# The end of attention's first batch in a fused attention and mixture-of-experts kernel: last steps packed closer, token weights moved behind them, a third output tile begun early

## The chip, the cores and the metric

The kernel runs on one core of a Trainium2 chip. A core has a matrix engine (TensorE, PE in the rows; PEld are its weight loads), three elementwise engines (VectorE, DVE; ScalarE, ACT; GpSimd, POOL) and a queue that issues transfers (SyncE, SP). Each works through its own list in order and waits on semaphores for the others. The metric is the device time of one execution in microseconds (us), the median of several runs.

## The reference

Attention over 2 batches of 8 heads, 576 positions, head size 64: heads 0 to 3 see the last 32 positions ("local"), heads 4 to 7 every 32nd ("strided"). Its output, as a matrix of 1152 tokens by 512, goes through four experts and a gated layer:

```python
attn_out = _attn_ref(**attn_kwargs)                 # softmax(q k^T / 8, masked) v
x = attn_out.transpose(0, 2, 1, 3).reshape(B * S, H * D)
p = domain_probs / (domain_probs.sum(-1, keepdims=True) + 1e-09)
for e in range(E):
    out += p[:, e:e+1] * (np.maximum(x @ w1[e], 0.0) @ w2[e])
gate = 1 / (1 + np.exp(-(out @ w_gate)))
return (gate * (out @ w_val) @ w_out)
```

All is float32. The kernel keeps a float32 value as two parts that TensorE takes, a high and a low one, and makes a product of three matmuls: high by high, low by high, high by low.

## The kernel before

**Attention in groups.** `attention` makes 16 groups of one batch, half a head each (kind `s` strided or `l` local, `c` the pair of heads, `half`, `hh` the head in the pair). A group goes through scores and mask on TensorE (tile `sps`), a row maximum on VectorE (`nm`), the exponentials on ScalarE (`P`, with the row sums in `sm`), the norm (two short VectorE operations on `sm`, a `TENSOR_SCALAR` and a `RECIPROCAL`, and a multiplication of `P` on GpSimd), a transposition on TensorE (`tps`) with a copy to `PT` on VectorE, and the product with the values on TensorE (`o`), for two groups at a time. The split takes `o` apart into the high part `xh` (a `CAST`) and the low part `xl` (a subtraction) of x, separately for each tile of 384 tokens. The software pipeline is by steps: group n starts at step n, `STAGES` (L46) says how many steps later each stage comes, and `attention` emits what falls into a step, stage by stage. The order of the stages in a step is that of `STAGES`, values first. `DRAIN` (L51) is the number of empty steps between the two batches.

**Buffers.** `o` has a PSUM bank of its own, one; only the last local `o` of each batch (half 1, c 1) is taken from the pool `gp`. That pool has four banks (`PSUM_BUFS`, L33), which also hold `tps`, `qkps` (transposed q and k), `warm`, `pps` and the output tiles `gps`.

**Split and weights.** From step `WEIGHTS_FROM` (L50) to `FIRST_GROUPS` both halves of a split are on VectorE; in other steps ScalarE copies `o` to `of` first and GpSimd makes the low part. From that step the weights of the first layer are prepared as well, one `early_step` or two behind each group: ScalarE casts 512 columns (`wh`), GpSimd subtracts (`wl`).

**The seam.** After the first 21 steps the units begin: `early_up` of the first tile of tokens makes four output tiles (fb 0 to 3) of 12 matmuls, over four blocks of x (kk); blocks 2 and 3 are strided heads, 0 and 1 local ones. `head_start` makes the six matmuls of blocks 2 and 3 in advance, at steps 17 and 18 (`HEAD_START`), for two of the four tiles. `keep_warm` puts matmuls on zeros into TensorE's list (`EMPTY`: how many in which step). `token_weights` and `spread_token_weights` normalise the token weights `ptok`, transpose them (`pps`), store them to DRAM (`pd`) and load them spread over the partitions (`p00`, first used by `early_down`). In the units, attention's second batch goes on between the matmuls: every product of three counts 0.36 of a step (`ATT_RATE`), so the places are fixed by the program's text, not by time.

Of the kernel before, what the change touches and what calls it, by code (L numbers as in the profile page):

```python
# [9 lines left out]
F32 = mybir.dt.float32  # L10
# [7 lines left out]
ALU = mybir.AluOpType  # L18
# [14 lines left out]
PSUM_BUFS = 4  # L33
PB_BUFS = 5
WARM = 11
EMPTY = {0: 2, 1: 4, 2: 2, 3: 2, 4: 2, **{i: 2 for i in range(5, 16, 2)}, 16: 1, 19: 1, 20: 1}
T_BUFS = 4
STEP_US = dict(early_up=0.53, early_down=0.53, expert_up=0.49, expert_down=0.49, gated_up=0.25, gated_down=0.65)
MARGIN = 5.5
# [5 lines left out]

STAGES = (("values", 5), ("transpose", 3), ("scores", 0), ("exp", 0), ("norm", 1), ("split", 5))  # L46
QUAD = 4
FIRST_GROUPS = 21
PT_BUFS = 5
WEIGHTS_FROM = 12  # L50
DRAIN = 5  # L51
HEAD_START = (17, 18)
ATT_RATE = 0.36


# [51 lines left out]
def attn_moe_glu_kernel(ctx, tc, q, k, v, dp, w1, w2, wg, wv, wo, out):  # L107
    nc = tc.nc
    ledger = Ledger()
    dve, act, pool_ = (Reckoned(e_, name, ledger) for e_, name in ((nc.vector, "V"), (nc.scalar, "A"), (nc.gpsimd, "G")))  # L110
    B, H, S, D = q.shape
# [8 lines left out]
    NU = S // 8  # L120
# [42 lines left out]
    def load_strided_v(b, c):  # L163
        h0 = 4 + 2 * c
        t = atp.tile([NU, 2, 8 * D], F32, tag="vs", name="vs", bufs=2)
        nc.sync.dma_start(t, v[b, h0:h0 + 2].rearrange("h (u r) d -> u h (r d)", r=8))
        qkv["vs", b, c] = t
# [38 lines left out]
    for e in range(EARLY // 2, E):  # L206
        for w_, name in ((w1, "w1"), (w2, "w2")):
            parts = []
# [11 lines left out]
    at = prep_order.index(item_of["wo", 0])  # L220
# [69 lines left out]
    def token_weights():  # L290
        dve.tensor_reduce(psums, ptok, AX.X, ALU.add)
        dve.tensor_scalar(psums, psums, 1e-9, None, ALU.add)
        dve.reciprocal(psums, psums)
        dve.tensor_tensor(ptok, ptok, psums.unsqueeze(2).to_broadcast([128, NTB, E]), ALU.mult)

    def spread_token_weights():
        ps = gp.tile([128, 512], F32, tag="g", name="pps")
        nc.tensor.transpose(ps[:NTB * E, :128], ptok.rearrange("p t e -> p (t e)"), ident)
        t = atp.tile([128, 288], F32, tag="PT", name="ptokT", bufs=PT_BUFS)
        ptokT = t[:NTB * E, :128]  # L300
        dve.tensor_copy(ptokT, ps[:NTB * E, :128])
        nc.sync.dma_start(pd, ptokT)
        load_p(0, 0, p00)
# [3 lines left out]
    def load_p(e, T, t):  # L307

        m = TC // 128
        src = pd.rearrange("(t e) p -> e t p", e=E)[e, m * T:m * T + m, :]  # L310
        nc.sync.dma_start(t, bass.AP(src.tensor, src.offset, [[0, 128], [E * 128, m], [1, 128]]))
        pb[e, T] = t.rearrange("p a b -> p (a b)")


    xh, xl = {}, {}
# [5 lines left out]
    def x_parts(b, lo, hi):  # L321

        done = lo
        while done < hi:
            T, o = divmod(b * S + done, TC)
            n = min(hi - done, TC - o)
            yield T, o, done, n
            done += n
# [336 lines left out]
    pt_tiles, of_tiles, soft = {}, {}, {}  # L665

    def qk_strided(b, c, hhs):

        for hh in hhs:
            for nm, dst in (("qs", QT), ("ks", KT)):  # L670
                src, t = qkv[nm, b, c], atp.tile([128, 4, NU], F32, tag=nm + "T", name=nm + "T", bufs=3)
                dst["s", b, c, hh] = t
                ps = gp.tile([128, 512], F32, tag="g", name="qkps")
                pv_ = ps[:, :4 * NU].rearrange("p (a b) -> p a b", b=NU)
                for rp in range(4):
                    nc.tensor.transpose(  # L676
                        pv_[:, rp, :], src[:, hh, rp * 128:(rp + 1) * 128], ident[:NU, :NU]
                    )
                if nm == "qs":
                    act.activation(t, pv_, AF.Copy, scale=SCALE)  # L680
                else:
                    dve.tensor_copy(t, pv_)
        if hhs[-1] == 0:
            return
        if (b, c) == (0, 1):
            alloc_x(NT - 1)
        if (b, c) == (1, 1):
            acc["x2"] = accp.tile([128, KC, NTOK], F32, tag="acc", name="x2acc")
# [73 lines left out]
    def group_values(g):  # L762
# [10 lines left out]
        for j in range(m):  # L773
            for x in range(2):
# [7 lines left out]
                )  # L782
        if at_step[0] in range(WEIGHTS_FROM, FIRST_GROUPS):
            of_tiles[g] = o, o
# [2 lines left out]
        act.copy(of, o[:, :288])  # L787
        of_tiles[g] = o, of

    def group_split(g):  # L790

        kind, b, c, half, hh = g
        if hh == 0:
            return
        o, of = of_tiles.pop(g)
        low = dve if of is o else pool_
        if kind == "s":
            kk = 2 + c
            hv, ov = (t[:, :288].rearrange("p (a u) -> p a u", u=NU) for t in (o, of))
            for T, off, s0, n in x_parts(b, 0, S):  # L800
                u0, u1 = s0 // 8, (s0 + n) // 8
                sel = lambda t: t[T][:, kk, off:off + n].rearrange("p (u a z) -> p z a u", a=4, z=2)[:, half]
                dve.tensor_copy(sel(xh), hv[:, :, u0:u1])
                low.tensor_tensor(sel(xl), ov[:, :, u0:u1], sel(xh).bitcast(F32), ALU.subtract)
        else:
            for T, off, s0, n in x_parts(b, 288 * half, 288 * half + 288):
                p0 = s0 - 288 * half
                dh, dl = xh[T][:, c, off:off + n], xl[T][:, c, off:off + n]
                dve.tensor_copy(dh, o[:, p0:p0 + n])
                low.tensor_tensor(dl, of[:, p0:p0 + n], dh.bitcast(F32), ALU.subtract)  # L810

    at_step = [0]

    def attention():

        gs = []
        for b in range(B):
            gs += [("s", b, c, half, hh) for c in range(2) for hh in range(2) for half in range(2)]
            gs += [("l", b, c, half, hh) for half in range(2) for hh in range(2) for c in range(2)]
        n = len(gs)  # L820
        stage = dict(values=group_values, transpose=group_transpose, scores=pair_scores,
                     exp=group_exp, norm=group_norm, split=group_split)

        def later(x):
            return int(x % QUAD == QUAD - 1 and (x + 1) % (n // B) != 0)

        step_of = [x + DRAIN * (x // (n // B)) for x in range(n)]
        at_stage = {}
        for name, behind in STAGES:
            for x in range(n):  # L830
                if name in ("values", "split"):
                    if x % QUAD >= 2:
                        at_stage[name, step_of[x] + behind + later(x)] = gs[x]
                elif name == "scores":
                    if x % 2 == 0:
                        at_stage[name, step_of[x]] = gs[x:x + 2]
                else:
                    at_stage[name, step_of[x] + behind] = gs[x]
        qk_strided(0, 0, (0,))
        for i in range(step_of[-1] + STAGES[-1][1] + 1):  # L840
            at_step[0] = i
            for name, _ in STAGES:
                if (name, i) in at_stage:
                    stage[name](at_stage[name, i])
            if i == 0:
                qk_strided(0, 0, (1,))
            if i in HEAD_START:
                head_start(HEAD_START.index(i))
            if i in EMPTY:
                keep_warm(EMPTY[i])  # L850
            for b in range(B):
                at = i - step_of[b * n // B]
                if b and at in (-5, -3):
                    qk_strided(b, 0, (int(at == -3),))
                if at in (2, 3):
                    qk_strided(b, 1, (at - 2,))
                if at in (6, 7, 9):
                    qk_local(b, (6, 7, 9).index(at))
            yield i
# [21 lines left out]
    def head_start(fb):  # L881

        head[fb] = g_tile()[:, :TC]
        for _ in split_products(head[fb], early_pairs(0, 0, fb, (2, 3)), last=False):
            pass
# [326 lines left out]
    def early_step(n):  # L1212
        ledger.now = max(ledger.now, ledger.done)
        prep_step(n)
# [28 lines left out]
    with tc.manual_schedule():  # L1243
# [12 lines left out]
        def attend():  # L1256

            i = next(att, None)
            if i == 0:
                load_strided_qk(1, 0)  # L1260
                load_raw_to(2)
            if i == 6:
                load_raw_to(3)
                load_strided_qk(1, 1)
            if i == 9:
                load_strided_v(1, 0)
            if i == 11:
                load_local(1)
            if i == 13:
                load_strided_v(1, 1)  # L1270
            if i == 18:
                token_weights()
            if i == 19:
                spread_token_weights()
            if i == 20:
                load_vl(1)
            return i

        att = attention()
        for i in range(FIRST_GROUPS):  # L1280
            attend()
            for _ in range((i >= WEIGHTS_FROM) + (i > 15)):
                early_step(0)
        n_none, n_step = 0, [0]
        halves = job(x_half())
# [103 lines left out]
```

## Time and profile before

| | us |
|---|---|
| runs | 650.26, 650.40, 650.83 |
| median | 650.40 |
| the profiled execution's own time | 651.06 |
| its span, first to last instruction | 648.9 |
| TensorE busy in it | 638.2 (98%) |

A row of the timeline has the start in us from the span's start, the time, engine, line, operation, output and input tiles, shape and count; in square brackets the idle time just before it and who ended it. The end of a matmul is modelled, and matmuls overlap, so the distance of two starts says more than the time of one. Line L101 is a helper that records every operation of VectorE, ScalarE and GpSimd, so those are told apart by their tiles.

### The profile page before, as it was taken

Reading aid. Unit: us, or ns where it says so; the run is one execution under the profiler, and the core shown is the slowest. Engines: PE = TensorE matmul, PEld = TensorE weight load, DVE = VectorE, ACT = ScalarE, POOL = GpSimd, SP = SyncE. Lnnn points to the kernel's source line nnn. Section 1 sums busy time; section 2 is a strip of 40 time slices with the busy share of each in tenths; the row PEclk is TensorE's granted clock in tenths of the full one; section 3 lists DMA queues with packets and bytes.
Section 4 is the critical chain, followed back from the end, with each engine's and each line's share of the span. In section 5 each row is a group of like instructions: output and inputs, shape, how many; then the busy total and the mean of one; then the engine's idle time right before and its main releaser. Section 6 shows DMA issues by size and latency. Waiting matters only on the chain.

```text
span 648.9 us, 12702 instructions
## 1 busy us (share of the span) xinstructions
PE 638.2 (98%) x4899; PEld 469.3 (72%) x4904; DVE 440.3 (68%) x885; ACT 341.7 (53%) x807; POOL 265.5 (41%) x307
## 2 busy tenths in 40 slices
PE   8889999999999999999999999999999999999998
PEld 5668889999676666666666666666979877987794
DVE  4876586787461886693887788898866659633432
ACT  5747553554854646774645554642565574532230
POOL 3665561000422226361335335440465377453540
PEclk9999999999999999999999999999999999999999
DMA  9965141030421544251664464354113832330002
GB/s 184 243 172 141 35 117 43 1 115 17 142 86 57 158 147 159 81 182 59 183 255 143 163 227 147 98 162 146 35 34 117 286 142 81 107 132 1 33 19 97
DMA packets 48884, 77.00 MB, mean 119 GB/s; under 512 B 19540, under 2 KB 24440, under 8 KB 47672
## 3 DMA queue, kind: packets, MB, share of 16 engines
q1 hardware_dynamic: 48824, 76.20, 37.6%
q8 instruction: 38, 0.62, 0.4%
q14 instruction: 22, 0.18, 0.1%
HBM read 59.66 MB, written 16.53 MB: 117 GB/s over the span
## 4 chain that ended last, share of the span: by engine, by line
PE 94%; DVE 1%; DMA 1%; SPq 1%; ACT 1%; issue 0%; POOL 0%; POOLq 0%; ACTq 0%
PE gps L874 23%; PE gps L876 23%; PE gps L875 23%; PE gps L976 19%; SPq L173 1%; PE sps L730 1%; PE warm L264 1%; PE tps L756 1%; PE o L780 1%; DMA ks<-in_k_dram 1%; ACT P L101 1%; DMA kl<-in_k_dram 1%; PE qkps L698 0%; PE qkps L676 0%; PE sps L717 0%; DVE nm L101 0%
## 5 line engine op out<-in xcount | busy, mean ns | idle before, releaser
L101 POOL TENSOR_TENSOR hl<-t,hh 128x384 f16<-128x384 f32 x72 | 76.5, 1065 | 179.2 <-ACT t L101 175.4
L976 PEld LDWEIGHTS <-w 128*128 128x128 f16 x1512 | 125.0, 98 | 1.8
L976 PE MATMUL gps<-x,w 128*128 128x192 f16 x1512 | 126.2, 246 | 0.0
L874 PE MATMUL gps<-x,w 128*128 128x384 f16 x288 | 93.9, 326 | 0.0
L875 PE MATMUL gps<-x,w 128*128 128x384 f16 x288 | 93.9, 326 | 0.0
L876 PE MATMUL gps<-x,w 128*128 128x384 f16 x288 | 93.9, 326 | 0.0
L874 PE MATMUL gps<-hh,w 128*128 128x384 f16 x288 | 93.9, 326 | 0.0
L875 PE MATMUL gps<-hl,w 128*128 128x384 f16 x288 | 93.9, 326 | 0.0
L876 PE MATMUL gps<-hh,w 128*128 128x384 f16 x288 | 93.9, 326 | 0.0
L874 PEld LDWEIGHTS <-w 128*128 128x128 f16 x576 | 56.4, 98 | 37.3 <-issue 0.2
L876 PEld LDWEIGHTS <-w 128*128 128x128 f16 x576 | 56.4, 98 | 37.2
L875 PEld LDWEIGHTS <-w 128*128 128x128 f16 x576 | 56.4, 98 | 36.4
L101 ACT ACTIVATE hh<-gps 128x384 f16<-128x384 f32 (+1 forms) x96 | 46.8, 487 | 48.8 <-PE gps L876 48.5
L101 POOL TENSOR_TENSOR stage<-magn,stage 128x512 f16<-128x512 f32 x36 | 45.5, 1273 | 45.1 <-ACT magn L101 38.9
L101 ACT ACTIVATE w<-raw,up 128x512 f16<-128x512 f32 x48 | 32.0, 715 | 34.8 <-DVE up L101 34.7
L101 ACT ACTIVATE P<-sps,nm 72x72 f32<-72x72 f32 (+1 forms) x112 | 36.4, 333 | 23.8 <-DVE sm L101 17.0
L101 ACT ACTIVATE bits<-raw 128x512 f32<-128x512 f32 x36 | 24.3, 674 | 38.1 <-DVE magn L101 37.9
L101 DVE SCALAR_TENSOR_TENSOR w<-raw,up,w 128x512 f16<-128x512 f32 x48 | 40.1, 871 | 5.1 <-ACT w L101 4.9
L101 POOL TENSOR_TENSOR sg<-four,sg 128x384 f32<-128x384 f32 x9 | 9.6, 1069 | 80.8 <-DVE four L101 77.9
L874 PE MATMUL gps<-w,hh 128*128 128x512 f16 (+1 forms) x112 | 41.6, 371 | 0.0
L875 PE MATMUL gps<-w,hh 128*128 128x512 f16 (+1 forms) x112 | 41.6, 371 | 0.0
L876 PE MATMUL gps<-w,hl 128*128 128x512 f16 (+1 forms) x112 | 41.6, 371 | 0.0
(145 smaller groups left out, 1281.5 us busy)
## 6 DMA issues: line engine op xcount, KB each, us to landing
raw<-in_moe_w_dram SPq DMA_DIRECT2D x32, 512.0 KB
raw<-in_moe_w_gate_dram SPq DMA_DIRECT2D x12, 512.0 KB
raw<-in_moe_w_val_dram SPq DMA_DIRECT2D x12, 512.0 KB
raw<-in_moe_w_out_dram SPq DMA_DIRECT2D x12, 512.0 KB
wg<-stage SPq DMA_DIRECT2D x21, 256.0 KB
wv<-stage SPq DMA_DIRECT2D x21, 256.0 KB
w<-wg SPq DMA_DIRECT2D x3, 1024.0 KB
wo<-stage SPq DMA_DIRECT2D x12, 256.0 KB
```

The lines of the kernel that those rows point to most:

```text
L101: return f(*a, **k)
L173: nc.sync.dma_start(t[:, :, j, :], src[b, 2 * j:2 * j + 2].rearrange("h s d -> (h s) d").rearrange("(c p) d -> p c d", p=128),)
L264: nc.tensor.matmul(ps, zero.to_broadcast([128, 128]), zero.to_broadcast([128, 512]), start=True, stop=True,)
L730: nc.tensor.matmul(pv_[:, j, :], qs_, ks_, start=False, stop=j == m - 1)
L756: nc.tensor.transpose(pv_[:, j, :], pp[:, j, :], ident[:n, :n])
L780: nc.tensor.matmul(o[x * 64:x * 64 + 64, j * n:(j + 1) * n], lhsT, tts[x][:, j, :], start=True, stop=True)
L874: nc.tensor.matmul(ps, ah, bh, start=first and i == 0, stop=False)
L875: nc.tensor.matmul(ps, ah, bl, start=False, stop=False)
L876: nc.tensor.matmul(ps, al, bh, start=False, stop=last and i == n - 1)
L976: nc.tensor.matmul(o, l_, r_, start=first and x + kk + y == 0, stop=last and x * kk * y == 2, skip_group_check=True)
```

## The change

- The first batch's last groups are packed. The `o` of c 1, half 0 comes one step after that of c 0 (step 16, not 17), the two of half 1 both in step 18 (not 19 and 20), the two last transpositions in steps 16 and 17. `DRAIN` goes from 5 to 3 and `FIRST_GROUPS` from 21 to 19.
- `group_split` takes several groups and goes by tiles of tokens first: the parts of the first 384 tokens of both `o`, then the rest.
- Three tiles are begun in advance, two in step 17 and one in step 18.
- Token weights are made in step 20 and spread in step 21, inside the first unit. The load of the second batch's local values (`vl`) moves from step 20 to 18.
- `WEIGHTS_FROM` goes from 12 to 11, so that the split of step 11 moves wholly to VectorE; weight preparation starts a step earlier and skips step 15: ten steps up to the units, where there were fourteen.
- The warm-up matmuls of steps 19 and 20 go, step 16 has two for one.
- The strided q and k of the second batch are transposed three and one steps ahead of it (five and three before): steps 16 and 18 as before.

```diff
-EMPTY = {0: 2, 1: 4, 2: 2, 3: 2, 4: 2, **{i: 2 for i in range(5, 16, 2)}, 16: 1, 19: 1, 20: 1}
+EMPTY = {0: 2, 1: 4, 2: 2, 3: 2, 4: 2, **{i: 2 for i in range(5, 17, 2)}, 16: 2}
-FIRST_GROUPS = 21
+FIRST_GROUPS = 19
-WEIGHTS_FROM = 12
-DRAIN = 5
-HEAD_START = (17, 18)
+WEIGHTS_FROM = 11
+DRAIN = 3
+HEAD_START = {17: (0, 1), 18: (2,)}
...
+    def group_split(*gs):
...
+        tiles = [of_tiles.pop(g) for g in gs]
+        for T, off, s0, n in parts:
+            for g, (o, of) in zip(gs, tiles):
+                low = dve if of is o else pool_
...
+                dve.tensor_copy(sel(xh), src(o))
+                low.tensor_tensor(sel(xl), src(of), sel(xh).bitcast(F32), ALU.subtract)
...
+        m = n // B
+        for name, x, i in (("values", m - 5, m), ("split", m - 5, m), ("transpose", m - 2, m), ("transpose", m - 1, m + 1),
+                           ("values", m - 2, m + 2), ("values", m - 1, m + 2), ("split", m - 2, m + 2), ("split", m - 1, m + 2)):
+            at_stage = {k_: g for k_, g in at_stage.items() if k_[0] != name or g != gs[x]}
+            moved.append((name, i, gs[x]))
...
-            if i in HEAD_START:
-                head_start(HEAD_START.index(i))
+            for fb in HEAD_START.get(i, ()):
+                head_start(fb)
...
-                if b and at in (-5, -3):
-                    qk_strided(b, 0, (int(at == -3),))
+                if b and at in (-3, -1):
+                    qk_strided(b, 0, (int(at == -1),))
...
+            if i == 20:
+                token_weights()
+            if i == 21:
+                spread_token_weights()
             if i == 18:
-                token_weights()
-            if i == 19:
-                spread_token_weights()
-            if i == 20:
                 load_vl(1)
...
-            for _ in range((i >= WEIGHTS_FROM) + (i > 15)):
+            for _ in range((i >= WEIGHTS_FROM) + (i > 15) - (i == 15)):
                 early_step(0)
```

TensorE's list at steps 15 to 17, before (-) and after (+); `qkps` are the second batch's q and k, and the row ahead of this piece is the `tps` of step 15, ahead of that the `o` of c 0, half 0:

```order
 L264 MATMUL warm<-const-float32-0.0 128x512
-L756 MATMUL tps<-ident,P 128x96 x3
+L780 MATMUL o<-PT,vl 64x96 x6
+L756 MATMUL tps<-ident,P 128x96 x6
+L264 LDWEIGHTS const-float32-0.0
+L264 MATMUL warm<-const-float32-0.0 128x512
 L264 LDWEIGHTS const-float32-0.0
 L264 MATMUL warm<-const-float32-0.0 128x512
 L676 MATMUL qkps<-ident,qs 128x72 x4
 L676 MATMUL qkps<-ident,ks 128x72 x4
-L780 MATMUL o<-PT,vl 64x96 x6
 L756 MATMUL tps<-ident,P 128x96 x3
```

The second `o` now stands ahead of the transposition, the warm-up and the eight `qkps` matmuls that stood between it and the first.

VectorE's list at steps 11 and 12, before:

```order
L101 CAST xh0_171<-o_575 128x4x48
L101 CAST xh1_173<-o_575 128x4x24
L101 COPY PT_619<-tps_615 128x288
L101 TENSOR_REDUCE nm_631<-sps_621 96x3
L101 TENSOR_SCALAR sm_593<-sm_593 96x3
```

and after:

```order
L101 CAST xh0_171<-o_575 128x4x48
L101 TENSOR_TENSOR xl0_172<-o_575,xh0_171 128x4x48
L101 CAST xh1_173<-o_575 128x4x24
L101 TENSOR_TENSOR xl1_174<-o_575,xh1_173 128x4x24
L101 COPY PT_620<-tps_616 128x288
L101 TENSOR_REDUCE nm_632<-sps_622 96x3
L101 TENSOR_SCALAR sm_591<-sm_591 96x3
```

Two subtractions came in ahead of the copy, the maximum and the sums. GpSimd's list over steps 11 to 15, before:

```order
L101 TENSOR_TENSOR xl0_172<-of_584,xh0_171 128x4x48
L101 TENSOR_TENSOR xl1_174<-of_584,xh1_173 128x4x24
L101 TENSOR_TENSOR P_594<-P_594,sm_593 96x384
L101 TENSOR_TENSOR P_633<-P_633,sm_632 96x384
L101 TENSOR_TENSOR wl_642<-raw_230,wh_641 128x512
L101 TENSOR_TENSOR P_661<-P_661,sm_660 96x384
L101 TENSOR_TENSOR P_697<-P_697,sm_696 96x384
L101 TENSOR_TENSOR wl_642<-raw_230,wh_641 128x512
```

and after:

```order
L101 TENSOR_TENSOR P_592<-P_592,sm_591 96x384
L101 TENSOR_TENSOR wl_614<-raw_230,wh_613 128x512
L101 TENSOR_TENSOR P_634<-P_634,sm_633 96x384
L101 TENSOR_TENSOR P_660<-P_660,sm_659 96x384
L101 TENSOR_TENSOR wl_614<-raw_230,wh_613 128x512
L101 TENSOR_TENSOR P_696<-P_696,sm_695 96x384
```

The two subtractions left it, and each `wl` stands one norm earlier.

TensorE's list at the end of the last tile begun in advance, before (the second tile, step 18):

```order
L874 MATMUL gps_794<-xh0_171,wh_641 128x384
L875 MATMUL gps_794<-xl0_172,wh_641 128x384
L876 MATMUL gps_794<-xh0_171,wl_642 128x384
L676 MATMUL qkps_802<-ident_97,qs_226 128x72 x4
L676 MATMUL qkps_809<-ident_97,ks_227 128x72 x4
L780 MATMUL o_824<-PT_717,vl_164 64x96
L780 MATMUL o_824<-PT_775,vl_164 64x96
```

and after (the third tile, step 18; both `o` of half 1 stand ahead of it, `gps_784` is tile 0 going on):

```order
L888 MATMUL gps_822<-xh0_171,wh_613 128x384
L889 MATMUL gps_822<-xl0_172,wh_613 128x384
L890 MATMUL gps_822<-xh0_171,wl_614 128x384
L676 MATMUL qkps_830<-ident_97,qs_226 128x72 x4
L676 MATMUL qkps_837<-ident_97,ks_227 128x72 x4
L888 MATMUL gps_784<-xh0_171,wh_613 128x384
```

The two `qkps` now come when three tiles begun in advance and one `o` hold `gp`'s four banks; before, two tiles held two.

## Rows read from the trace of the kernel before

**Rows 1.** Busy us (instructions) by stretch: PE, PEld, DVE, ACT, POOL; granted clock, DMA, GB/s.
```profile
25.00:70.00 45.00, 39.56 (x402) 32.82 (x404) 32.19 (x94) 27.66 (x124) 27.67 (x32) 1.00 0.62 160
70.00:640.00 570.00, 570.00 (x4227) 417.74 (x4226) 391.03 (x738) 297.20 (x597) 226.89 (x251) 1.00 0.34 112
```
**Rows 2.** TensorE's timeline, 29 to 45 us.
```profile
29.84 0.60 PE L264 MATMUL warm<-const-float32-0.0 128*128 128x512 bf16 x2
31.07 0.47 PE L756 MATMUL tps<-ident,P 96*128 96x96 f32 x3 [0.63 <-POOL P L101]
...
32.89 0.72 PE L780 MATMUL o<-PT,vl 128*64 128x96 f32 x12 [0.20 <-PE sps L730]
...
33.84 0.38 PE L264 MATMUL warm<-const-float32-0.0 128*128 128x512 bf16 x1
34.95 0.47 PE L756 MATMUL tps<-ident,P 96*128 96x96 f32 x3 [0.72 <-POOL P L101]
...
35.72 0.41 PE L676 MATMUL qkps<-ident,ks 72*128 72x72 f32 x4
36.23 0.72 PE L780 MATMUL o<-PT,vl 128*64 128x96 f32 x12
...
38.85 0.47 PE L756 MATMUL tps<-ident,P 96*128 96x96 f32 x3 [0.42 <-POOL P L101]
39.10 0.42 PE L874 MATMUL gps<-xh,wh 128*128 128x384 f32 x1
...
40.24 0.41 PE L676 MATMUL qkps<-ident,qs 72*128 72x72 f32 x4
40.49 0.42 PE L676 MATMUL qkps<-ident,ks 72*128 72x72 f32 x4
...
43.15 0.27 PE L298 MATMUL pps<-ident,ptok 128*36 128x128 f32 x1 [1.26 <-DVE ptok L101]
...
44.36 0.38 PE L264 MATMUL warm<-const-float32-0.0 128*128 128x512 bf16 x1 [0.29 <-DVE ptokT L101]
```
**Rows 3.** VectorE's timeline, 28 to 53 us.
```profile
28.07 0.65 DVE L101 CAST xh<-o 128x192 fp32r<-128x192 f32 x2
28.55 0.44 DVE L101 COPY PT<-tps 128x288 f32<-128x288 f32 x1
...
31.17 0.47 DVE L101 CAST xh<-o 128x192 fp32r<-128x192 f32 x1
...
32.70 0.45 DVE L101 COPY PT<-tps 128x288 f32<-128x288 f32 x1
...
34.97 0.17 DVE L101 TENSOR_SCALAR sm<-sm 96x3 f32<-96x3 f32 x1
...
35.72 0.46 DVE L101 TENSOR_TENSOR xl<-o,xh 128x288 fp32r<-128x288 f32 x1
...
36.52 1.07 DVE L101 TENSOR_SCALAR sm<-sm 96x3 f32<-96x3 f32 x1
...
42.92 0.24 DVE L101 CAST xh<-o 128x96 fp32r<-128x96 f32 x1
...
44.03 0.27 DVE L101 COPY ptokT<-pps 36x128 f32<-36x128 f32 x1
...
52.78 0.56 DVE L101 SCALAR_TENSOR_TENSOR hl<-gps,hh 128x384 fp32r<-128x384 f32 x1 [1.53 <-ACT hh L101]
```
**Rows 4.** GpSimd's timeline, 29 to 38 us.
```profile
29.10 1.08 POOL L101 TENSOR_TENSOR xl<-of,xh 128x192 fp32r<-128x192 f32 x2
30.19 0.82 POOL L101 TENSOR_TENSOR P<-P,sm 96x384 f32<-96x384 f32 x1
...
36.29 1.28 POOL L101 TENSOR_TENSOR wl<-raw,wh 128x512 fp32r<-128x512 f32 x1
```
**Rows 5.** ScalarE's timeline at 40.7 us: the copy of transposed q out of `qkps`.
```profile
40.69 0.41 ACT L101 ACTIVATE qsT<-qkps 128x288 f32<-128x288 f32 x1 [2.94 <-PE qkps L676]
```
**Rows 6.** TensorE's timeline at the start: the first eleven warm-up matmuls.
```profile
0.78 4.81 PE L264 MATMUL warm<-const-float32-0.0 128*128 128x512 bf16 x11 [0.78 <-PEq L1374]
```

More of the change, by code (lines that the diff above doesn't have):

```diff
@@ L788, in group_values @@
         of_tiles[g] = o, of
-    def group_split(g):
-        kind, b, c, half, hh = g
-        if hh == 0:
+    def group_split(*gs):
+        for kind, b, c, half, hh in gs:
+            break
+        else:
             return
-        o, of = of_tiles.pop(g)
-        low = dve if of is o else pool_
         if kind == "s":
[L798 to L804, printed above, removed]
-        else:
[L806 to L810, printed above, removed]
+            parts = x_parts(b, 0, S)
+        else:
+            parts = x_parts(b, 288 * half, 288 * half + 288)
+        tiles = [of_tiles.pop(g) for g in gs]
+        for T, off, s0, n in parts:
+            for g, (o, of) in zip(gs, tiles):
+                low = dve if of is o else pool_
+                if kind == "s":
+                    kk, u0, u1 = 2 + g[2], s0 // 8, (s0 + n) // 8
+                    sel = lambda t: t[T][:, kk, off:off + n].rearrange("p (u a z) -> p z a u", a=4, z=2)[:, half]
+                    src = lambda t: t[:, :288].rearrange("p (a u) -> p a u", u=NU)[:, :, u0:u1]
+                else:
+                    p0 = s0 - 288 * half
+                    sel = lambda t: t[T][:, g[2], off:off + n]
+                    src = lambda t: t[:, p0:p0 + n]
+                dve.tensor_copy(sel(xh), src(o))
+                low.tensor_tensor(sel(xl), src(of), sel(xh).bitcast(F32), ALU.subtract)
     at_step = [0]
@@ L827, in attention @@
         step_of = [x + DRAIN * (x // (n // B)) for x in range(n)]
-        at_stage = {}
+        at_stage, moved = {}, []
         for name, behind in STAGES:
@@ L844, in attention @@
                     stage[name](at_stage[name, i])
+                both = [g for name_, i_, g in moved if (name_, i_) == (name, i)]
+                if name == "split":
+                    group_split(*both)
+                else:
+                    for g in both:
+                        stage[name](g)
             if i == 0:
                 qk_strided(0, 0, (1,))
-            if i in HEAD_START:
-                head_start(HEAD_START.index(i))
+            for fb in HEAD_START.get(i, ()):
+                head_start(fb)
             if i in EMPTY:
```

## The prediction, as put on record

> **What bounds the kernel now.** Read the windows first [rows 1]. From 70 us TensorE is busy 570.00 of 570.00 us at a granted clock of 1.00, so nothing that another engine does there sets the end, and the three products of every value are the same matmuls before and after. What the change can win or lose lies ahead of 70 us: TensorE is busy 39.56 of 45 us between 25 and 70. All of the idle time gone would be 5.4 us, the most that can be won there, and each microsecond added there goes through to the end, since no idle time is left behind it to take it up. The chain of waits that ended last says the same: it is matmuls nearly all the way, so I read TensorE's timeline next [rows 2], and for each idle time in brackets the engine that ended it [rows 3 to 5].
>
> The reader should see three kinds of wait there. The transpositions `tps` at 31.07, 34.95 and 38.85 us wait for GpSimd's norm (0.63, 0.72, 0.42 us). The `o` at 36.23 starts 0.05 us after VectorE's subtraction on the same bank ended (35.72 + 0.46 = 36.18), and 0.26 us later than the matmuls ahead of it would have let it (35.72 + 0.25, the distance of the two `qkps` at 40.24 and 40.49). And `pps` waits 1.26 us for the token weights, the `warm` behind it 0.29 us.
>
> **What the change takes away.** The warm-ups fall from four to three in these steps, and two pairs differ from one by 0.60 - 0.38 = 0.22 us: 0.22. The waits of `pps` and the `warm` behind it leave this place: 1.26 + 0.29. The wait of the `o` in front of its bank (0.26) and those of the two `tps` (0.72 and 0.42) go because the waits below stand ahead of them or in their place. Together 3.17 us.
>
> **What it adds, step by step.**
>
> Step 11. VectorE had two casts ahead of the copy `PT`, 28.55 - 28.07 = 0.48 us; now it has casts and subtractions, which cost 32.70 - 31.17 = 1.53 us one split later [rows 3]. Everything behind them (maximum, sums, norm, transposition) is 1.05 us later. In return GpSimd loses 1.08 us of `xl`, which the norm `P` at 30.19 had waited behind [rows 4]. The relief only helps if `P` is not then waiting for VectorE; its input comes from the list that has just become longer. Between 0 and 1.05; I take 0.7, nearer the price of the four operations.
>
> VectorE behind `wl`. A `TENSOR_SCALAR` on `sm` costs 0.17 us at 34.97 and 1.07 us at 36.52, and the second lies inside GpSimd's `wl` (36.29 to 37.57) and ends with it [rows 3, 4]. The subtraction of 0.46 us at 35.72, out of PSUM, is not stretched. After the change each `wl` stands one norm earlier, right behind the `P` that VectorE's own previous sums released: it runs from about 0.9 to 2.2 us behind those sums (a `P` of 0.82, then 1.28), and the next group's sums (36.52 - 34.97 = 1.55 us apart here) fall into it at steps 13 and 15. Each can lose 0 to 1.1 us; for the pair 0 to 2.2, I take 1.5, since the one case seen lost 0.9. The Trainium skill, page "SBUF — State Buffer", section "Who interferes with whom", says that VectorE and GpSimd share a port pair that one instruction holds to its end, and that `tensor_scalar` can need it, while an operation with one SBUF input outside the two-port modes does not. By that rule both meetings cost in full and the sum would be 0.7 us more; the two rows agree with it.
>
> The second `o`. All local `o` but the last share one bank. The next one waits until VectorE has taken the one before apart. Start of `o` to end of `xl` was 36.18 - 32.89 = 3.29 us [rows 2, 3]. Before, a `tps`, two `warm`, another `tps` and eight `qkps` stood between. Now there is `o` and `tps` (33.84 - 32.89 = 0.95 us) and two warm-ups of 0.22: 1.39 us. The wait is 1.9 us, 1.7 at the least if VectorE comes a little sooner. This is the term I trust most: the bank is one, the place in the list is given.
>
> The transposition of step 17. It needs the norm of a group whose sums come only a step earlier, and VectorE's list is now 1 to 2 us late while TensorE has less to do ahead of it. The nearest rows are waits of 0.42 to 0.72 us with the old distance [rows 2]; a step nearer, the whole chain of sums, reciprocal and `P` (0.17 + 0.17 + 0.82) shows. 0.9 to 1.3, I take 1.1.
>
> Four banks. Three tiles begun in advance and the one `o` of step 18 hold all of `gp`. The first `qkps` behind them waits until VectorE has taken both `o` apart, in eight operations; four cost 44.03 - 42.92 = 1.11 us, so about 2.3 us from the end of the first `o`. TensorE has under it the second `o` and the third tile's six matmuls (40.24 - 39.10 = 1.14 us), so 0.5 to 1.1 us are open. The second `qkps` has again no free bank and waits for ScalarE's copy of the first, 0.41 us [rows 5] and the ways there and back, 0.4 to 0.7. Sum 0.9 to 1.8, I take 1.6.
>
> `pps` in the unit. Moved to the first unit it takes a bank that is released only by a low part `hl`, and `hl` at 52.78 stands behind a wait of 1.53 us for ScalarE [rows 3]. What TensorE loses of that is between 0.3 and 1.5; I take 0.9, the middle, since no row is nearer to either end.
>
> Weights. With ten preparation steps for fourteen, at least two `wl` of 1.28 us go into the first units, where GpSimd also has the norms of the second batch. Hidden if the units' matmuls ahead cover them, else up to half of the pair: 0 to 1.3, I take 0.5. `vl` earlier and the token weights' transfers behind the weight loads on SyncE cost nothing as long as the first use of `p00`, in `early_down`, is later than their landing; the DMA engines' share is 0.62 in this stretch and 0.34 behind it [rows 1], so there is room, and I price it at 0 and leave its failure to the range.
>
> The sum: 0.7 + 1.5 + 1.9 + 1.1 + 1.6 + 0.9 + 0.5 = 8.2 added, 3.17 removed: 5.0 us net. The profiled execution took 651.06 us, 0.66 more than the median of the runs, 650.40. So 656.1 against that execution, and 655.4 on the runs' basis. All low ends give 0 + 0 + 1.7 + 0.9 + 0.9 + 0.3 + 0 = 3.8, net 0.6; all high ends 1.05 + 2.2 + 1.9 + 1.3 + 1.8 + 1.5 + 1.3 = 11.05, net 7.9.
>
> **The rivals.** *Faster.* The second `o` hardly waits. Its bank is free once the cast and the subtraction, twice some 0.46 us, have followed the end of the first `o` (0.72 us after its start): 1.64 us, if VectorE had nothing else to do, against 1.39 us of work ahead, a wait of 0.25. If VectorE's list is ahead by then (GpSimd's relief at step 11 outweighs the four operations, no sums fall into a `wl`), then the other waits stand at their low ends too: 0.25 + 0.5 for the transposition + 0.9 + 0.3 = 1.95, less 3.17, net -1.2: 649.2. It decides at an added sum under 3.17. Against it: VectorE reached that cast at about 35.72 - 0.46 = 35.26, some 1.65 us after the `o` ended (32.89 + 0.72), with a copy and sums ahead of it (34.97), and its list has become longer, not shorter. Chance 0.08.
>
> *No difference.* The change does what it says in the order of the lists, but waits only change places: the 5.4 us of idle time are spread over fewer steps, the sums miss `wl`, the banks come free in time. That is near the low ends, net -1.3 to +1.3: 650.4. The windows speak for it so far as the matmuls are the same; the two structural waits (second `o`, banks) speak against. Chance 0.06.
>
> *Slower still, by the clock.* The granted clock is 1.00 through waits of up to 1.26 us. The first eleven warm-ups, at the start, took 4.81 us, 0.44 each [rows 6], and later 0.22: the level of 1.2 GHz for that of 2.4. A gap of 1.9 us or more, with waits of about 1 us on both sides, has no row here. If the clock falls there, the `o`, `tps`, warm-ups and `qkps` behind it, some 2.2 us, and perhaps the tiles begun in advance take double: 2 to 4 us, I take 3: 658.4. The Trainium skill, page "TensorE: Matmul & The Clock Gate", section "HAM oscillation — how this bites in real kernels", describes such a fall behind idle stretches; the trace of before shows none. Chance 0.10.
>
> **How the numbers follow.** My forecast, net +5.0, has 0.76, so 655.4 us. The range is to hold the time 8 times in 10: from 652.2 (between the sum of low ends, 651.0, and the forecast) to 657.8 (the high ends give 658.3, part of the clock's rival lies within). Left out are the faster and the equal rival (0.14) and the upper half of the clock's. A measurement here can tell about 0.2%, 1.3 us, from no change. Slower by more than that: 0.76 + 0.10 = 0.86; within it 0.06; faster 0.08.
>
> **What would show it.** In the new trace TensorE should be idle nearly 2 us or more ahead of the `o` of step 16, ended by VectorE's `xl`; one or two `TENSOR_SCALAR` on `sm` of about 1 us should lie inside a `wl`; the first `qkps` behind the third tile should wait about 1 us and the second 0.5 us or so; `pps` should wait for `hl`; and from about 75 us TensorE should again be busy throughout. If the `o` of step 16 starts without a wait, the largest term is wrong and with it the sign may be; if the clock shows less than 1.00 behind it, the third rival holds.

## The result, and the profile after

The changed kernel took 660.3 us (659.7 to 661.2 in four executions), before 650.6 in the same comparison: a ratio of 1.0149, interval 1.0131 to 1.0166. It is 9.7 us slower. The direction was forecast, the size was not: 5.0 us were forecast, and the time lies above the range (652.2 to 657.8).

The profiled execution took 660.36 us, with a span of 658.5 against 648.9. Read its windows beside [rows 1]; the columns are the same.

```profile
25.00:70.00 45.00, 35.67 (x318) 29.04 (x317) 27.66 (x81) 21.94 (x96) 20.83 (x23) 0.89 0.60 158
70.00:110.00 40.00, 38.51 (x353) 32.94 (x353) 26.62 (x77) 21.45 (x92) 23.98 (x31) 1.00 0.26 78
110.00:640.00 530.00, 530.00 (x3915) 386.89 (x3915) 365.27 (x676) 280.32 (x531) 206.24 (x221) 1.00 0.35 115
```

Two things are new. TensorE is idle 9.3 us between 25 and 70 us, where it was 5.4, and another 1.5 between 70 and 110. And the granted clock between 25 and 70 us is 0.89, not 1.00. From 110 us on TensorE is busy throughout, so all that is lost lies ahead of that; the forecast had this from about 75 us on, and the wait of 1.39 us at 81.72 lies behind that.

TensorE's timeline of the changed kernel, the rows with a wait of 0.5 us or more and two rows behind the longest; to be read against [rows 2].

```profile
30.31 0.72 PE L780 MATMUL o<-PT,vs 72*64 72x72 f32 x16 [0.86 <-DVE xl L101]
...
35.34 0.72 PE L780 MATMUL o<-PT,vl 128*64 128x96 f32 x12 [1.41 <-issue]
...
39.77 1.23 PE L780 MATMUL o<-PT,vl 128*64 128x96 f32 x12 [2.88 <-DVE xl L101]
40.92 1.22 PE L756 MATMUL tps<-ident,P 96*128 96x96 f32 x6
...
43.97 0.74 PE L756 MATMUL tps<-ident,P 96*128 96x96 f32 x3
...
51.34 0.44 PE L676 MATMUL qkps<-ident,qs 72*128 72x72 f32 x4 [0.81 <-DVE xl L101]
52.28 0.47 PE L676 MATMUL qkps<-ident,ks 72*128 72x72 f32 x4 [0.50 <-ACT qsT L101]
...
61.45 0.29 PE L298 MATMUL pps<-ident,ptok 128*36 128x128 f32 x1 [1.24 <-DVE hl L101]
...
81.72 0.44 PE L890 MATMUL gps<-xh,wl 128*128 128x384 f32 x1 [1.39 <-POOL wl L101]
```

The `o` at 39.77 is that of step 16. It takes 1.23 us where the same twelve matmuls took 0.72 in [rows 2]. The windows of the changed kernel at the fall and at the return (stretch, TensorE's busy time, granted clock, DMA share, GB/s):

```profile
36.00:37.00 1.00, 0.89 (x7) 1.00 0.75 168
37.00:37.50 0.50, 0.00 (x0) 0.72 0.85 188
37.50:38.00 0.50, 0.00 (x0) 0.50 1.25 274
...
44.00:47.40 3.40, 3.40 (x12) 0.50 0.00 0
47.40:50.00 2.60, 2.60 (x32) 0.99 0.00 0
```

The clock falls from 2.4 to 1.2 GHz some 0.3 us into the gap ahead of that `o`, and returns at 47.4 us. From 39.77 to 47.4 are 7.6 us of work at the lower level. How much of that is lost is not simply half: the matmuls of one output tile start 0.32 us apart there and 0.17 to 0.18 behind it, so the run e1_warm below has to say it.

The stretched sums on VectorE, and GpSimd's `wl` beside them, to be read against [rows 3] and [rows 4]:

```profile
32.33 1.18 DVE L101 TENSOR_SCALAR sm<-sm 96x3 f32<-96x3 f32 x1
...
37.40 1.17 DVE L101 TENSOR_SCALAR sm<-sm 96x3 f32<-96x3 f32 x1
...
39.16 0.46 DVE L101 TENSOR_TENSOR xl<-o,xh 128x288 fp32r<-128x288 f32 x1
```

```profile
32.22 1.27 POOL L101 TENSOR_TENSOR wl<-raw,wh 128x512 fp32r<-128x512 f32 x1
...
37.29 1.26 POOL L101 TENSOR_TENSOR wl<-raw,wh 128x512 fp32r<-128x512 f32 x1
```

Each begins inside a `wl` (32.22 to 33.49, 37.29 to 38.55) and ends with it. Behind the first the whole split of step 13 is late, and the `o` at 35.34 waits 1.41 us for its bank; the profile names no releaser there, but VectorE's last `xl` on that bank ended 0.1 us before. Behind the second `xl` ends at 39.62, and the `o` at 39.77 follows.

### The profile page after: what moved, and what is told of

Same layout as the page of the kernel before. It is cut to its first block, busy times and chain, and to the rows that moved or that the text cites. A ratio compares the mean times of both kernels' runs of the same rounds, so it can differ in the third digit from the quotient of the medians.

```text
span 658.5 us, 12699 instructions
## 1 busy us (share of the span) xinstructions
PE 642.9 (98%) x4903; PEld 472.4 (72%) x4903; DVE 439.7 (67%) x887; ACT 341.6 (52%) x806; POOL 264.4 (40%) x305
## 4 chain that ended last, share of the span: by engine, by line
PE 94%; DVE 3%; ACT 1%; issue 1%; POOL 0%; POOLq 0%; ACTq 0%
PE gps L888 23%; PE gps L890 23%; PE gps L889 22%; PE gps L990 19%; PE sps L730 2%; PE tps L756 2%; PE o L780 1%; PE warm L264 1%; PE qkps L676 1%; ACT P L101 1%; DVE nm L101 1%; PE sps L717 1%; DVE sm L101 1%; DVE xh L101 0%; PE qkps L698 0%
```

## The experiments

Two theories stood against each other: that the loss is the forecast's list of waits with the clock on top, each with its own place, or that the waits only pass one lateness on, so that undoing one hands it to the next, and the clock's slow work covers waits that would be there anyway. Each kernel below is the changed one with the edit shown, unless it says otherwise, and was compared with the kernel before on the same chip.

One thing on reading single executions: they differ by up to 1.1 us before the first scores (`sps`) start, at 5.33 us in the profile of x_bank and at 6.39 in that of the changed kernel. From there to the transposition at about 27 us (27.33 in the kernel before) the distance is 21.4 us in every profile. So a difference of under 1 us between two profiles is taken below from the first `sps` to the last matmul.

**The clock, e1_warm.** Warm-up matmuls fill the two long gaps.

```diff
-EMPTY = {..., **{i: 2 for i in range(5, 17, 2)}, 16: 2}
+EMPTY = {..., **{i: 2 for i in range(5, 17, 2)}, 14: 6, 15: 12, 16: 2}
```

> The changed kernel with warm-up matmuls in its two idle gaps: six at step 14 (none there now), twelve at step 15 instead of two. Everything else is as changed. Theory: of the 9.7 us lost, about 5 are waits and the rest is the clock, which fell to half 0.5 us into the gap of 2.88 us ahead of the second o and came back 7.6 us of work later. With TensorE busy in the gaps the clock stays at 1.00, the second o starts where it did (39.8 us), the 7.6 us of work take 3.8, and of that about 1 us comes back as a wait of the transposition of step 17: 2.7 to 3.8 us less, 656.5 to 657.6 us. Rival, the slow work only covers waits that would have been there anyway: at most 1 us less, 659.3 to 660.3.

It took 657.7 us (ratio 1.0108, 1.0093 to 1.0123), 2.6 less than the changed kernel. Its window and the transposition of step 17:

```profile
25.00:70.00 45.00, 38.29 (x365) 1.00 0.57 151
```

```profile
42.98 0.47 PE L756 MATMUL tps<-ident,P 96*128 96x96 f32 x3 [1.00 <-POOL P L101]
```

The clock stays up in this stretch, and 1.00 us comes back where the changed kernel has no wait (43.97 above). The price of the fall is the distance from the `o` of step 16 to the next `o`, in the changed kernel (to 48.07) and here (39.68 to 45.52):

```profile
48.07 1.21 PE L780 MATMUL o<-PT,vl 128*64 128x96 f32 x24
```

```profile
39.68 0.72 PE L780 MATMUL o<-PT,vl 128*64 128x96 f32 x12 [0.69 <-DVE xl L101]
...
45.52 1.21 PE L780 MATMUL o<-PT,vl 128*64 128x96 f32 x24
```

That is 8.30 us against 5.84, and 1.00 of the 5.84 is the wait. So the fall costs 3.5 us, of which 1.0 covers a wait: net 2.5, against 2.6 measured, by addition of work and no removal of any. The rival is out.

**The second o a step later, e2_o17.**

```diff
-("values", m - 5, m), ("split", m - 5, m)
+("values", m - 5, m + 1), ("split", m - 5, m + 1)
```

> The changed kernel with one step undone: the o of c 1, half 0 and its split go back from step 16 to step 17. Theory: the wait of 2.88 us ahead of that o is the single bank (1.9) and VectorE's stretched sums (1.0); with the o a step later the bank part goes, and the transposition now first in the list waits for GpSimd's norm, behind the same stretched sums, about 2 us. Waits down by 1 us, and if the clock stays up with gaps of 2 us, 2.7 to 3.8 more: 655.5 to 656.6; if it still falls, 659.3. Rival, the bank is no cause and VectorE's lateness is passed on whole: a gap of 2.9 us ahead of the transposition, clock down, 660.3.

658.8 us (1.0123, 1.0108 to 1.0138). The gap of 2.88 us is gone; in its place the first transposition waits:

```profile
39.00 0.74 PE L756 MATMUL tps<-ident,P 96*128 96x96 f32 x3 [1.26 <-POOL P L101]
```

That is less than the 2 us expected, but it does not decide against the rival (the lateness passed on whole). The clock fell all the same, and earlier, at 32 us, in the middle of work, with gaps of only 0.85 and 0.45 us ahead of it:

```profile
31.00:32.00 1.00, 0.55 (x6) 1.00 0.92 219
32.00:33.00 1.00, 1.00 (x8) 0.53 1.04 215
```

So the work ahead of the transposition ran at the lower clock and covers part of its wait: `o`, `tps` and two warm-ups take 2.55 us here (34.51 to 37.06) where the prediction's rows have 1.39, and at that speed the wait would have been about 2.5 us (an estimate). The second stretched sum also took only 0.46 us here. How much of the lateness is passed on, x_bank shows. The time lies between what the theory gave with the clock up (655.5 to 656.6) and down (659.3), nearer to the latter; of the 1.5 us less, 0.8 stand ahead of the first `sps` in the profiled executions, and 0.7 behind it. The long gap is not needed for the fall.

**The split of step 11 back on GpSimd, e3_split12.**

```diff
-        if at_step[0] in range(WEIGHTS_FROM, FIRST_GROUPS):
+        if at_step[0] in range(12, FIRST_GROUPS):
```

> The changed kernel with one part undone: the split of step 11 stays with ScalarE's copy and GpSimd's low part, as before; weights still begin at step 11. Theory: the o of step 13 (30.31 us) waited 0.86 us for VectorE's last subtraction on its bank; with the copy the bank comes free early and that wait goes. 0.6 to 0.9 us less, 659.4 to 659.7, the two stretched sums, the gap of 2.9 us and the fall of the clock staying as they are. Rival, GpSimd's low part pushes the norm back and the wait goes over to the transposition: 660.3, a tps wait of over 1 us at 32 us.

659.45 us (1.0132, 1.0117 to 1.0147): 0.85 less by the medians, which alone is within the two intervals. The trace is clearer: from the first `sps` on it is 0.8 us shorter. The wait of 0.86 us ahead of the `o` of step 13 is gone, the transposition behind it waits 0.62, and the next `o` waits 1.41 as in the changed kernel:

```profile
30.79 0.47 PE L756 MATMUL tps<-ident,P 96*128 96x96 f32 x3 [0.62 <-POOL P L101]
33.82 0.72 PE L780 MATMUL o<-PT,vl 128*64 128x96 f32 x12 [1.41 <-issue]
```

So the wait was the bank: with ScalarE's copy the bank comes free early, with VectorE's two-step split it is held to the last subtraction.

**The weights at their old steps, e4_wl.**

```diff
-            for _ in range((i >= WEIGHTS_FROM) + (i > 15) - (i == 15)):
+            for _ in range((i >= 12) + (i > 15)):
```

> The changed kernel with the preparation of weights at the steps of before (from step 12 on, step 15 not left out): as many steps ahead of the units, ten, each a norm later. Theory: the two TENSOR_SCALAR of 1.18 and 1.17 us on sm are VectorE standing against GpSimd's wl; now they miss it or one meets it at most, the waits of 1.41 and 2.88 us shrink to about 0.4 and 1.9, 2 us less, 658.3 if the clock still falls. If it stays up with a gap of 1.9 us, 2.7 to 3.8 more: 654.5 to 655.6. Rival, the sums are late for another reason (the row sums of ScalarE): both stay above 1 us, 660.3.

Median 657.9 us (1.0112, 1.0075 to 1.0149), with the widest scatter of all: 655.38 in an execution with a mean clock of 1.000, 657.83 and 657.90 with 0.992, 660.62 with 0.990. The sums take 0.17 us, the wait of 1.41 us is gone (0.40 is left of it in w_wl below, at the higher clock), that of 2.88 is 1.79. The profiled execution was one with 0.992. Its timeline of TensorE and its windows:

```profile
29.30 0.72 PE L780 MATMUL o<-PT,vs 72*64 72x72 f32 x16 [0.87 <-DVE xl L101]
...
31.30 0.47 PE L756 MATMUL tps<-ident,P 96*128 96x96 f32 x3 [0.45 <-POOL P L101]
...
37.70 0.72 PE L780 MATMUL o<-PT,vl 128*64 128x96 f32 x12 [1.79 <-DVE xl L101]
```

```profile
31.00:31.50 0.50, 0.20 (x2) 1.00 0.81 201
31.50:32.00 0.50, 0.50 (x5) 0.66 0.82 204
32.00:32.50 0.50, 0.50 (x4) 0.50 1.11 259
...
35.00:36.00 1.00, 0.92 (x7) 0.97 0.72 155
...
38.50:39.00 0.50, 0.50 (x5) 0.50 1.24 272
```

It fell twice: behind waits of 0.87 and 0.45 us, and again behind that of 1.79. The sums' part of the theory holds; what it gave for the clock up, 654.5 to 655.6, is what the one undisturbed execution shows.

**The same with the clock held, w_wl.**

```diff
-EMPTY = {..., 16: 2}
+EMPTY = {..., 12: 3, 13: 4, 15: 9, 16: 2}
...
-            for _ in range((i >= WEIGHTS_FROM) + (i > 15) - (i == 15)):
+            for _ in range((i >= 12) + (i > 15)):
```

> The changed kernel with the weights at the steps of before (from step 12 on, step 15 not left out), and warm-ups that fit into the gaps which e4_wl showed: three at step 12, four at 13, nine at 15. It asks for the price of the two stretched sums with the clock held. The execution of e4_wl whose clock stayed at 1.00 took 655.4 us, e1_warm with the sums stretched 657.7. Theory: clock 1.00, both TENSOR_SCALAR at 0.15 to 0.17 us, 655.3 to 655.9 and less scatter than e4_wl (655.4 to 660.6). Rival, the scatter of e4_wl was not the clock but the transfers: again 655 to 660.

655.6 us (1.0083, 1.0067 to 1.0098); three of four executions between 655.35 and 655.66 at a clock of 1.000, one at 0.997 with 657.46. Against e1_warm, 2.1 us less. TensorE's row of the second `o`, and VectorE's sums at that place:

```profile
37.53 0.72 PE L780 MATMUL o<-PT,vl 128*64 128x96 f32 x12 [0.33 <-DVE xl L101]
```

```profile
36.17 0.17 DVE L101 TENSOR_SCALAR sm<-sm 96x3 f32<-96x3 f32 x1
```

That is the price of the two stretched sums, 2.0 us by the rows (1.18 and 1.17 for 0.17 each). Seven more warm-ups of 0.22 us and the wait of 0.33 are 1.87 us: the second `o`'s own wait, without the sums.

**The bank, x_bank.** w_wl with the `o` of step 16 in `gp`, and two warm-ups at step 15 as in the change.

```diff
-        if half and (kind, c) == ("l", 1):
+        if (half or not b) and (kind, c) == ("l", 1):
...
-EMPTY = {..., 12: 3, 13: 4, 15: 9, 16: 2}
+EMPTY = {..., 12: 3, 13: 4, 15: 2, 16: 2}
```

> w_wl with the o of step 16 in a bank of gp, not in the one bank of the local o, and without the seven warm-ups that filled its wait at step 15. It asks whether that bank is what the second o waits for. Theory: in w_wl that wait is 0.33 us behind seven warm-ups of 0.22, 1.87 together; with a bank of its own the o starts at once. The transpositions behind it then come to their norms earlier, so that one or two of them wait about 1.1 us: 0.6 to 1.0 us less than w_wl, 654.6 to 655.0, clock up. Rival, the o waits for its transposed P or the values instead: an o wait of 1 us or more remains, 655.6.

Median 655.8 us (1.0073, 1.0059 to 1.0086), but one execution stayed at a clock of 1.000 with 653.99 us, the three others at 0.997. The `o` no longer waits, and the transpositions do. The profiled execution is the one at 1.000:

```profile
36.73 0.47 PE L756 MATMUL tps<-ident,P 96*128 96x96 f32 x3 [0.89 <-POOL P L101]
...
39.17 0.47 PE L756 MATMUL tps<-ident,P 96*128 96x96 f32 x3 [0.76 <-POOL P L101]
```

It is 1.5 us below w_wl's 655.5, but 0.9 of that stands ahead of the first `sps` (5.33 us, 6.20 in w_wl). From there on it gains 0.8 us, as expected, and more than half of the bank's 1.87 us goes over to the norms: the bank is what the `o` waited for, and the lateness is passed on in part. The three executions at 0.997 took 655.8 to 656.6 us, no less than w_wl; where their clock fell was not traced.

**Four banks, w_two.** e1_warm with two tiles begun in advance.

```diff
-HEAD_START = {17: (0, 1), 18: (2,)}
+HEAD_START = {17: (0,), 18: (1,)}
```

> e1_warm with two tiles begun in advance (steps 17 and 18) in place of three. It asks for the price of gp's four banks. Theory: the first qkps behind the tiles no longer waits for the split of both o (0.81 us), and the place of the third tile's six matmuls moves into the unit at no cost; the wait of the second (0.50, ScalarE's copy) goes too if a bank is free. 0.8 to 1.3 us less than e1_warm, 656.4 to 656.9. Rival, the pps in the unit waits that much longer for a bank: 657.7.

656.8 us (1.0088, 1.0074 to 1.0102; 655.45 to 656.86), 0.9 less. The 0.81 us ahead of the first `qkps` are gone, the 0.50 ahead of the second are not, and `pps` waits longer (1.24 above):

```profile
57.22 0.40 PE L298 MATMUL pps<-ident,ptok 128*36 128x128 f32 x1 [1.76 <-DVE hl L101]
```

The time is in the expected range and its parts are not: the rival's wait came in, 0.52 us, and the late weights' wait of 1.39 us went as well, with a `tps` wait of 0.58 in its stretch. And the clock fell at the end of the longer `pps` wait, at about 57.2 us, and was back at 60.6, in spite of the warm-ups. Below are a window of that stretch (columns as above), the first matmul on `hh` behind it, and the same matmul in x_all, which has the same tiles and the clock up:

```profile
58.00:59.00 1.00, 1.00 (x4) 0.50 0.00 0
```

```profile
61.41 0.44 PE L888 MATMUL gps<-hh,wh 128*128 128x384 f32 x1
```

```profile
55.83 0.44 PE L888 MATMUL gps<-hh,wh 128*128 128x384 f32 x1
```

From `pps` on that is 4.19 us (57.22 to 61.41), in x_all 2.69 (53.14 to 55.83): 1.5 us. So the 0.9 is what is left after a new fall, and the price of the banks alone was not isolated.

**Late weights, w_14.** e1_warm with fourteen preparation steps.

```diff
-            for _ in range((i >= WEIGHTS_FROM) + (i > 15) - (i == 15)):
+            for _ in range((i >= WEIGHTS_FROM) + 2 * (i > 15)):
```

> e1_warm with fourteen steps of weight preparation ahead of the units in place of ten (three at each of the steps 16 to 18, step 15 not left out). It asks for the price of late weights. Theory: the wait of 1.39 us in the second unit that ends with GpSimd's wl goes: 1.0 to 1.4 us less, 656.3 to 656.7. Rival, the casts are late for their transfers or stand in ScalarE's way at step 18, and something else waits: 657.7 or more.

656.3 us (1.0086, 1.0072 to 1.0100), 1.4 less than e1_warm, as expected. The wait on `wl` is gone. Since w_two lost it as well, with ten preparation steps, the count of steps is one way to remove it and not its only cause. Half a microsecond more stands at a `qkps` (0.22 in the changed kernel):

```profile
62.17 0.47 PE L676 MATMUL qkps<-ident,qk 72*128 72x72 f32 x4 [0.73 <-DVE hl L101]
```

**Five parts undone, x_all.** The edits of e2_o17, e3_split12 and w_two's tiles, with weights from step 12 and three each at steps 16 to 18, and the change's own warm-ups.

> The changed kernel with five parts undone together and the warm-ups as the change has them: o of c 1, half 0 at step 17, split of step 11 with GpSimd, weights from step 12 and three each at steps 16 to 18, two tiles begun in advance. What is left of the change: the last groups and token weights two steps closer to the units. Theory, the terms add up: 660.3 less the clock (2.6), the sums (2.1), the split (0.8), the banks (0.9), the late weights (1.4) and the second o (0.9) is 651.6, at a clock of 1.00: 650.8 to 652.0, no difference from before. Rival, something of the packing is still missing from the account: 653 or more, or the clock falls.

651.3 us (1.0017, 1.0007 to 1.0027). Eight of twelve executions have a clock of 1.000 and 650.55 to 651.49 us, four 0.997 and 652.85 to 653.60. The expectation had added the single results up to 651.6 us, so the parts come close to adding up. What remains of the change, the last groups two steps closer and the token weights in the unit, wins nothing: the transpositions now wait for the norm, the last `o` for its bank and `pps` for its bank.

```profile
36.38 0.47 PE L756 MATMUL tps<-ident,P 96*128 96x96 f32 x3 [0.97 <-POOL P L101]
...
40.80 1.21 PE L780 MATMUL o<-PT,vl 128*64 128x96 f32 x24 [0.41 <-DVE xl L101]
...
53.14 0.28 PE L298 MATMUL pps<-ident,ptok 128*36 128x128 f32 x1 [1.22 <-DVE hl L101]
```

**The weights alone in the kernel before, b4_wl.**

```diff
-            for _ in range((i >= WEIGHTS_FROM) + (i > 15)):
+            for _ in range((i >= 11) + (i > 15) - (i == 15)):
```

> The kernel of before with one part of the change alone: weights from step 11, step 15 left out, the split of step 11 as before. Theory: the next sums fall into wl as in the changed kernel, 1.0 us each at steps 13 and 15, while the one stretched sum of before (1.07 at 36.5 us) goes; the second o of before, which had 0.05 us to spare on its bank, then waits 1.0 to 1.5 us. Net 0.5 to 1.5 us more, 651.5 to 652.5 with the clock up; if it falls there, 654 to 656. Rival, in the looser order of before the stretched sums are hidden: 651.0.

653.7 us (1.0044, 1.0031 to 1.0057). The sums are stretched to 1.39 and 1.18 us, the first local `o` waits 1.40:

```profile
33.98 0.72 PE L780 MATMUL o<-PT,vl 128*64 128x96 f32 x12 [1.40 <-issue]
...
38.32 1.23 PE L780 MATMUL o<-PT,vl 128*64 128x96 f32 x12 [0.17 <-DVE xl L101]
```

```profile
36.00:40.00 4.00, 3.81 (x28) 0.50 0.98 227
```

The clock fell in this profiled execution (0.995 in the mean, 654.47 us); the one execution at 1.000 took 652.88. So this part alone, in the old order, costs some 2 us at full clock, more than the 0.5 to 1.5 expected, and brings the fall with it. That is one execution, but the rows agree: the second `o` starts 32.51 us behind the first `sps` (5.81), in the kernel before 30.31 (5.92 to 36.23), 2.2 us earlier, and both times VectorE's `xl` sets it. The second `o` waits only 0.17 us there, with the matmuls ahead of it at half the clock.

**Token weights alone in the kernel before, b2_tok.**

```diff
-            if i == 18:
+            if i == 21:
                 token_weights()
-            if i == 19:
+            if i == 22:
                 spread_token_weights()
```

> The kernel of before with one part of the change alone: the token weights are made and spread in the first unit, steps 21 and 22, in place of 18 and 19. Theory: the waits of 1.26 and 0.29 us for them at 43 us go, TensorE has 36 matmuls there under which VectorE's small operations lie; a wait of pps for its bank, or none, comes in. With two tiles in gp and not three the bank comes in time: 1.0 to 1.6 us less than before, 649.0 to 649.6. Rival, pps waits 1.24 us for hl as in the changed kernel: 650.0 to 650.6, no difference.

649.2 us (0.9979, 0.9971 to 0.9988): 1.4 us faster than before by the ratio (1.7 by the medians), at a clock of 0.999 to 1.000 in all eleven executions. It beats both kernels. `pps` has no wait, and VectorE's multiplication takes 0.20 us (it took 1.00 beside `wl`):

```profile
46.54 0.27 PE L298 MATMUL pps<-ident,ptok 128*36 128x128 f32 x1
```

```profile
45.99 0.20 DVE L101 TENSOR_TENSOR ptok<-ptok,psums 128x36 f32<-128x36 f32 x1
```

In x_all, which also begins two tiles in advance, `pps` waits 1.22 us for its bank; what in the packing makes that difference was not tried by itself.

## Why the prediction had the direction right and the time wrong

The terms beside what the rows and runs gave:

| term | forecast, us | measured, us |
|---|---|---|
| split of step 11 | 0.7 | 0.86 (the `o` at 30.31; gone in e3_split12) |
| two stretched sums | 1.5 | 1.01 + 1.00 = 2.01 (2.1 by w_wl against e1_warm) |
| second `o` | 1.9 | 1.87 (w_wl) |
| transposition of step 17 | 1.1 | 0 beside the slow clock, 1.00 with it up (e1_warm) |
| four banks | 1.6 | 0.81 + 0.50 = 1.31 |
| `pps` in the unit | 0.9 | 1.24 |
| late weights | 0.5 | 1.39 |
| two small waits in the unit | none | 0.18 + 0.22 |
| the clock | 0; 3 as a rival | 3.5 of slow work, 2.5 net (e1_warm) |

Without the clock the rows add to 9.1 us against 8.2 forecast; with it 12.6, and less the 3.17 removed 9.4, against 9.7 measured. That this fits so well is in part chance. Waits of 0.35, 0.24 and 0.58 us in the units of the kernel before went too, which the prediction did not count. And the profiled execution was 0.5 us later already at its first `sps`, ahead of anything that the change touches: the two `qkps` in front of it took longer than before, as long as those in the slow stretch at 42.79 (0.69 us). Before, and in the changed kernel:

```profile
5.42 0.42 PE L676 MATMUL qkps<-ident,qs 72*128 72x72 f32 x4
```

```profile
5.43 0.68 PE L676 MATMUL qkps<-ident,qs 72*128 72x72 f32 x4
```

**The step that failed is the clock.** It stands in the sum at 0, and its fall cost 3.5 us of slow work, 2.5 net; with the clock held the time is 657.7 (e1_warm), just inside the range. The prediction had its price nearly right (3 us, 2 to 4) and its place, but set it beside the forecast, as another case with a chance of 0.10, though its condition was a term of the forecast itself: it said that a wait of 1.9 us or more has no row in the trace of before, and then forecast that very wait. The clock belonged on top of 5.0 us with the chance that it has given that wait, not against it; and the range, which took only half of that rival in, would have had to reach about 660. The Trainium skill, page "TensorE: Matmul & The Clock Gate", section "HAM oscillation — how this bites in real kernels", describes idle stretches that bring the lower clock. The trace of the changed kernel agrees in kind (the fall 0.3 us into the gap of 2.88 us, 0.50 granted for 10.2 us); e2_o17 and e4_wl, where it fell in the middle of work, do not. What sets it off stays open.

**A second step sized too small: the sums.** The prediction took 1.5 of a possible 2.2 us for the pair. The Trainium skill, page "SBUF — State Buffer", section "Who interferes with whom", says that of two operations that need the shared ports the later one is blocked until the other ends. Both sums show it, at 1.18 and 1.17 us, each ending with its `wl`, so that rule was the better guide than the middle of the bounds. In e3_split12 and b4_wl a sum that starts 0.1 us ahead of its `wl` by the profile was stretched to the end of it too (1.37 and 1.39 us), so which came first cannot be read off the starts. Of the rows that the prediction leaned on, the subtraction at 35.72 ended at 36.18, ahead of that `wl` (36.29), so it shows nothing of a meeting with it.

**A third: late weights,** 1.39 us against 0.5. It lies just above the bounds (0 to 1.3), and w_14 takes the wait away with more steps, w_two with the same ten and one tile fewer begun in advance.

**Right value, wrong reason: the split of step 11.** It was argued over GpSimd's norm; the rows show the bank, held by VectorE's subtraction where ScalarE's copy had freed it early. The bank was the argument for the second `o` in the same text and was not carried to this place.

**Right:** TensorE is busy throughout behind the waits (from 82 us, not 75), so what is lost ahead goes through to the end; the second `o` (1.9 and 1.87); the transposition of step 17 (1.1 and 1.00, seen only with the clock up); the rivals of a gain and of no difference, of which nothing came.

## What to carry to other kernels

Where a sum of waits makes a gap longer than any in the trace, price the clock on top of the sum and not beside it. A part of a change may be worth more alone: token weights moved by themselves win 1.4 us, and the packing around them loses it. And the bank that ScalarE's copy freed early here was held to the last subtraction when VectorE took over the reading: look who waits for a bank before moving such work. Last, a held clock is not held everywhere: a wait made longer elsewhere (1.76 us in w_two) had a fall of its own.

## What had not been expected of the hardware

The clock's fall does not need the long gap. In e4_wl it fell at some 31.7 us, in the middle of work, behind waits of 0.87 and 0.45 us, where the changed kernel passed waits of 0.86 and 0.45 at 1.00; and executions of one kernel differ: e4_wl 655.4 to 660.6 us with mean clocks of 1.000 to 0.990, x_all 651.2 and 653.0 with 1.000 and 0.997. No run here shows what decides between them, so this stays open. What the runs do show is that some 2 to 4 us of warm-ups, placed in waits that are there anyway, kept the mean clock at 0.997 or more in every execution of e1_warm and w_wl, where the changed kernel had 0.989 to 0.995. That is not the same as no fall: all four executions of w_two have 0.997, and the profiled one has the fall at 57 us.
